# Seven products in place of eight for the middle group's second products, and one block's running sum kept in DRAM

## The chip, the core and the metric

One NeuronCore of a Trainium2 chip runs the whole kernel. The engines are TensorE (PE, matrix products), VectorE (DVE), ScalarE (ACT), GpSimd (POOL) and SyncE (SP, which issues most DMAs). SBUF is the working memory, PSUM holds what PE writes, DRAM is the main memory. The metric is the device time of one execution in microseconds (us), the median of several runs; lower is better.

## The reference

Three steps follow each other; the output is that of the last.

```python
# attention with decay: 2 batches, 8 heads, 768 tokens, 64 per head
state = gamma[None, :, None, None] * state + np.einsum('bhd,bhe->bhde', k[:, :, t], v[:, :, t])
y[:, :, t] = scale * np.einsum('bhd,bhde->bhe', q[:, :, t], state)
...
# first layer: x is 1536 x 512, w_gate and w_val 512 x 1536, w_out 1536 x 512
xn = x / rms * rms_g
g = xn @ w_gate
silu = g * (1.0 / (1.0 + np.exp(-g)))
x2 = (silu * (xn @ w_val)) @ w_out
...
# second layer: w_in is 512 x 2048, w_out 2048 x 512
h = x2 @ w_in
out = np.maximum(0.01 * h, h) @ w_out
```

## The kernel before

**Numbers in two parts.** The weights come in 64 bits and are converted on the chip, by ACT and DVE, to 32 bits and split into a high and a low part (the operations "P", "1" to "4", "H", "L" of `open_unit`). Every operand of a product is such a pair, and a product is three matmuls: high by high, high by low, low by high. A product of one column of 128 features with one block of 512 tokens is 12 matmuls of 128 x 512.

**Tiling.** The 1536 tokens are three blocks, b = 0, 1, 2. The features between two matrices go by columns f of 128, 12 in the first layer and 16 in the second. Columns go in groups of four: `groups` 0 to 2 are the first layer (kinds "gvo": w_gate, w_val, w_out), 3 to 6 the second (kinds "ip": w_in, w_out). First products (g, v, i) make a column's features; second products (o, p) take these features through w_out and add over a group's columns in four PSUM banks. At a group's end the banks go to SBUF.

**Seven products in place of eight.** Blocks 1 and 2 and two neighbouring columns form a 2 x 2 scheme in which seven products of sums replace eight (`quad` for first products, `seventh` for second ones). It needs sums and differences of weights (units named `sg4`, `sv4`, ...: "1" to "4", "H", "h", "L", "l" in `open_unit`), of inputs (`follow`), and additions of results (`put` in `seventh`). A product is then half as long: six matmuls. First products use it from column 2 of the first layer on. Second products use it in the groups of `seven`: before the change the last four, that is the second layer alone. The first layer's second products go the direct way: `down` makes one column by one block, `accumulate` adds over the group, and `evac1` empties the banks into `x2acc` (L660 by ACT in the first group, L662 by DVE in the others). When the last group is done, `evac1` queues the splitting of x2 into high (ACT, L665) and low parts (DVE, L668) in `sums`, from which two are taken at each step.

**Order.** `plan` writes out the order of all steps; a step's products and `later` work follow it. `run` takes the steps one by one; after each it makes the high and low parts of the next two columns (`upper`, `lower`, L611 and L619), and converts weights as long as estimated clocks of DVE and ACT stay behind that of PE. `wq` is the order in which weights are loaded and converted, `room` gives them one of 14 places, `free` and `used` give the place back. SP loads raw weights (L387) into three buffers, each free again when DVE has done step "3" (L468). Instructions then go to each engine's queue; a queue runs in order, but its order is not that of the text: what waits is placed later.

**What the change touches besides.** `more` is a tile of four 128 x 512 pieces. In the second layer `place` gives its pieces to block 0's features, and `evac2` copies block 0's sum of a group there (L796), which POOL adds to the output in DRAM (L800); `recall` reads the sum back before the last group's end (L816). `scratch` tiles, nine of them, hold the other features.

```python
    seven = set(range(len(groups) - SEVEN, len(groups)))
...
        for m in range(4):
            dst = acc[b][:, m, :]
            if gi == 0:
                nc.scalar.activation(out=dst, in_=banks[m], func=AF.Copy)
            else:
                nc.vector.tensor_tensor(out=dst, in0=banks[m], in1=dst, op=ALU.add)
```

Of the kernel before, what the change touches and what calls it, by code (L numbers as in the profile page):

```python
# [8 lines left out]
F32 = mybir.dt.float32  # L9
# [7 lines left out]
P = 128  # L17
# [9 lines left out]
LEFT = 2  # L27
HEAD = "dddd0"
OVER = 1.5
COST = {n: ("a", 1.2) if n == "P" else ("a", 0.54) if n == "H" else ("v", 0.34 if n in "12" else 0.6) for n in "P1234HL"}  # L30
COST_SUM = {n: ("a", 0.54) if n in "Hh" else ("v", 0.34 if n in "1234" else 0.6) for n in "123H4hLl"}
TWICE = "gvi"
SEVEN = 4
RAWS = 3
WARM = 7
# [27 lines left out]
def chain_kernel(ctx: ExitStack, tc: tile.TileContext, qk_t, kv, w1, w2, mask, qdec, kdec, sdec, rms_g, ident, out):  # L63
# [18 lines left out]
    scr = ctx.enter_context(tc.tile_pool(name="scr", bufs=SCRATCH))  # L82
    ps_acc = ctx.enter_context(tc.tile_pool(name="ps_acc", bufs=1, space=bass.MemoryType.PSUM))
    attn_pools = ctx.enter_context(ExitStack())
    score_pool = ctx.enter_context(ExitStack())
# [3 lines left out]
    sm = attn_pools.enter_context(tc.tile_pool(name="sm", bufs=4))  # L89

    mask_sb = const.tile([P, 2, NPAIR, CH], F32, name="mask_sb")
    qdec_sb = const.tile([P, NPAIR, CH], F32, name="qdec_sb")
# [256 lines left out]

    seven = set(range(len(groups) - SEVEN, len(groups)))  # L350

    def doubled(n, f):
        if n == "p":
            return any(f in groups[gi][1] for gi in seven)
        return n in TWICE and f"{n}{f}" not in PLAIN

    wq = []
    for gi, (kinds, fs) in enumerate(groups):
        pairs_of = [(n, f) for f in fs[::2] for n in kinds]
        if gi in seven:  # L360
            pairs_of.sort(key=lambda t: kinds.index(t[0]))
        for n, f in pairs_of:
            wq += [source(n, f), source(n, f + 1)]
            if doubled(n, f):
                wq.append((f"s{n}{f}", None))
# [25 lines left out]
    def open_unit():  # L391
# [12 lines left out]
        if src is None:  # L404
# [24 lines left out]

            if n == "p":  # L430
# [184 lines left out]
    def lower(key):  # L615
        if key in halves:
            x, h = halves.pop(key)
            l = gp.tile([P, 512], F32R, tag="gl", name="g{}_{}_{}l".format(*key))
            nc.vector.tensor_tensor(out=l, in0=x, in1=h.bitcast(F32), op=ALU.subtract)  # L619
            parted[key] = h, l  # L620
            spend("v", 0.6)
            if key[0] == "q":
                follow(key[1], key[2])
                spend("v", 0.6 if key[2] in (1, 3, 5, 6) else 0.0)
# [9 lines left out]
    def down(gi, f, b):  # L634
        kinds, fs = groups[gi]
        L = kinds[-1]
        key = (L, f, b)
        upper(key)
        lower(key)
        accumulate(L, gi, f, b, f == fs[0], f == fs[-1], L == "o" or b > 0)  # L640
        used(f"{L}{f}")
        if f == fs[-1]:
            banks = acc.pop("b")
            first = gi in (0, len(G1))
            by_copy = first or L == "p" and b == 0 and gi < len(groups) - 1
            later.append(("a" if by_copy else "v", 2.4, lambda: (evac1 if L == "o" else evac2)(gi, b, banks)))
        placed[0] = order.index(key) + 1

    def evac1(gi, b, banks):
        if gi == 0:  # L650
            acc[b] = xp.tile([P, 4, 512], F32, tag=f"acc{b}", name=f"x2acc{b}")
        last = gi == len(G1) - 1
        own = range(2, 4) if b == 2 else range(4)
        if last:
            x2h[b] = xp.tile([P, 4, 512], F32R, tag=f"xh{b}", name=f"x2h{b}")
            x2l[b] = xp.tile([P, 4, 512], F32R, tag=f"xl{b}", name=f"x2l{b}")
        for m in range(4):
            dst = acc[b][:, m, :]
            if gi == 0:
                nc.scalar.activation(out=dst, in_=banks[m], func=AF.Copy)  # L660
            else:
                nc.vector.tensor_tensor(out=dst, in0=banks[m], in1=dst, op=ALU.add)  # L662
        if last:
            def high(m):
                nc.scalar.activation(out=x2h[b][:, m, :], in_=acc[b][:, m, :], func=AF.Copy)  # L665

            def low(m):
                nc.vector.tensor_tensor(  # L668
                    out=x2l[b][:, m, :], in0=acc[b][:, m, :], in1=x2h[b][:, m, :].bitcast(F32), op=ALU.subtract
                )  # L670

            highs, lows = ([lambda m=m, do=do: do(m) for m in own] for do in (high, low))
            if b == 2:
                one, two = slice(0, 2), slice(2, 4)
                ops = sums_of(
                    acc, x2h, x2l, acc[1][:, one], acc[1][:, two], x2h[2][:, one], x2l[2][:, one], extra()[:, two]
                )
                first_of = [lambda i=i: [ops[n]() for n in (f"{i}", f"h{i}")] for i in range(4)]
                sums.extend(first_of[:2] + [ops["l1"]] + highs + [ops["l0"]] + lows)
                sums.extend([first_of[2], ops["l2"], first_of[3], ops["l3"]])  # L680
            else:
                sums.extend(highs + lows)

# [6 lines left out]

    def gather(gi):
        for f in groups[gi][1][::2]:
            t = {(k, b): made.pop(("p", f + k, b)) for k in range(2) for b in (1, 2)}
            made["q", f, 1], made["q", f, 3], made["q", f, 2] = t[0, 1], t[1, 2], t[1, 1]
            turns[f] = t

    turns = {}
    touched = set()

    def follow(f, n):  # L700
        t = turns[f]

        def less(out, in0, in1):
            nc.vector.tensor_tensor(out=out, in0=in0, in1=in1, op=ALU.subtract)

        if n == 1:
            less(t[0, 1], t[0, 2], t[0, 1])
            made["q", f, 5] = t[0, 1]
        elif n == 5:
            less(t[0, 1], t[1, 2], t[0, 1])  # L710
            made["q", f, 6] = t[0, 1]
        elif n == 6:
            less(t[0, 1], t[1, 1], t[0, 1])
            made["q", f, 4] = t[0, 1]
        elif n == 3:
            less(t[0, 2], t[1, 2], t[0, 2])
            made["q", f, 7] = t[0, 2]

    def seventh(gi, n, f):
        fs = groups[gi][1]  # L720
        key = ("q", f, n)
        if n == 1 and f == fs[0]:
# [6 lines left out]
        unit, half, side, start, (b, row) = SIDES[n]  # L729
        names = f"p{f}", f"p{f + 1}", f"sp{f}", f"sp{f + 1}"  # L730
        w = wt[names[unit]]
# [21 lines left out]
        if f != fs[-2]:  # L753
            return
        banks = acc[side]
        fresh = gi == len(G1) and (b, row) not in touched
        touched.add((b, row))
        if b not in y2:
            y2[b] = xp.tile([P, 4, 512], F32, tag=f"acc{b}", name=f"y2acc{b}")

        def put():
            for m in range(2):
                dst = y2[b][:, 2 * row + m, :]
                if fresh:
                    nc.scalar.activation(out=dst, in_=banks[m], func=AF.Copy)
                else:
                    nc.vector.tensor_tensor(out=dst, in0=banks[m], in1=dst, op=ALU.add)
# [116 lines left out]
    def place(n, key, own=None):  # L884

        if n == "v":
            return gates.pop(key)
        if n == "i" and key[1] == 0:
            return extra()[:, key[0] % 4, :]
        return scratch(f"{n}{key[0]}_{key[1]}") if own is None else own  # L890
# [45 lines left out]
    def quad(n, f):  # L936
# [5 lines left out]
        def kept_sum(m, src):  # L942
            def put():
                q[m] = scratch(f"{n}{m}_{f}")
                nc.scalar.activation(out=q[m], in_=src, func=AF.Copy)
# [53 lines left out]
    def plan():  # L999
# [12 lines left out]
        for gi, (kinds, fs) in enumerate(groups):  # L1012
# [19 lines left out]
            if first:  # L1032
                for n in HEAD:
                    if n == "d":
                        fill.pop(0)()
                    else:
                        f = fs[int(n)]
                        put((f"i{f}",), lambda f=f: whole("i", f, 0, x2h, x2l))
            if gi in seven:
                for f in fs[::2]:  # L1040
                    own = [fill.pop(0) for _ in range(min(2, len(fill)))]
                    for i7, (keys, step) in enumerate(quad("i", f)):
                        put(keys, step)
                        if i7 in BEHIND[2] and own:
                            own.pop(0)()
                wholes = [lambda f=f: put((f"i{f}",), lambda: whole("i", f, 0, h, l)) for k, f in enumerate(fs) if not first or str(k) not in HEAD]
                for n, more in zip((1, 5, 6, 3, 7, 2, 4), (1, 0, 1, 0, 1, 0, 1)):
                    for f in fs[::2]:
                        order.append(("q", f, n))
                        keys = (f"p{f}", f"p{f + 1}", f"sp{f}", f"sp{f + 1}")[SIDES[n][0]], "half"  # L1050
                        put(keys, lambda n=n, f=f, gi=gi: seventh(gi, n, f))
# [235 lines left out]
```

## Time and profile before

| | us |
|---|---|
| median of 3 runs | 582.85 (582.84 to 583.4) |
| the profiled execution | 583.3 |
| its span, first to last instruction | 581.3 |
| PE busy | 571.3 (98%) |
| DVE busy | 505.8 (87%) |
| ACT busy | 355.9 (61%) |
| POOL busy | 26.6 (5%) |

The profile is of one execution, and its own time is the one to compare with its span; around the span lie 2.0 us. TensorE's granted clock was 1.00 throughout. Attention takes the first 60 us or so, the first layer's products lie between about 70 and 338 us (the middle group between 141.5 and 234), the second layer's between 338 and 578. A busy time says how long an engine had an instruction in it, not that it worked at its best; "L" with a number is a line of the kernel printed above.

### The profile page before, as it was taken

The numbers are of one execution on the slowest core, as the hardware profiler recorded it, in microseconds if no ns is written. First come the engines' busy times: TensorE is split into PE (matmuls) and PEld (weight loads), VectorE is DVE, ScalarE is ACT, GpSimd is POOL, SyncE is SP. The second block draws the span as 40 slices with busy tenths as digits, with TensorE's granted clock in tenths as the row PEclk, the third lists the DMA queues.
The fourth block names the chain that finished last, engine by engine and source line by source line (L and its number), as shares of the span: only waits on it lengthen the run. The fifth ranks groups of instructions, "written<-read, shape, count | busy, mean of one in ns | idle before, by whom it ended". The sixth has DMA issues, their size and how long they took to land.

```text
span 581.3 us, 8448 instructions
## 1 busy us (share of the span) xinstructions
PE 571.3 (98%) x3107; PEld 471.1 (81%) x3107; DVE 505.8 (87%) x921; ACT 355.9 (61%) x652; POOL 26.6 (5%) x28
## 2 busy tenths in 40 slices
PE   7899999999999999999999999999999999999997
PEld 4788788888888888888888878888888888888885
DVE  4899999999578579697688999999999999997793
ACT  2689656776565464554564667877856885676330
POOL 2332100000000000000000000000000020002000
PEclk9999999999999999999999999999999999999999
DMA  8991240433222221221411111113411353111545
GB/s 327 408 392 59 73 144 1 145 110 115 67 73 73 72 74 31 78 72 38 144 37 36 38 36 37 57 53 108 173 39 43 109 142 78 36 37 19 127 85 133
DMA packets 34072, 56.97 MB, mean 98 GB/s; under 512 B 19184, under 2 KB 19312, under 8 KB 34032
## 3 DMA queue, kind: packets, MB, share of 16 engines
q1 hardware_dynamic: 32736, 54.34, 28.9%
q0 software_dynamic: 1152, 2.10, 2.5%
q8 instruction: 24, 0.39, 0.3%
q14 instruction: 16, 0.13, 0.1%
q10 hardware_dynamic: 144, 0.00, 0.0%
HBM read 50.14 MB, written 6.29 MB: 97 GB/s over the span
## 4 chain that ended last, share of the span: by engine, by line
PE 88%; DMA 6%; DVE 3%; ACT 2%; issue 1%; SPq 0%; POOL 0%; DVEq 0%; POOLq 0%; ACTq 0%
PE ao L603 17%; PE iX L931 8%; PE ap L603 7%; PE X L738 7%; PE i L574 7%; PE v L574 7%; PE g L574 6%; PE Z L738 6%; PE vX L931 5%; PE gX L931 5%; PE iZ L931 4%; PE vZ L931 2%; PE gZ L931 2%; DMA qkv<-in_qk_t 2%; PE iY L931 2%; DMA qkv<-in_kv 2%
## 5 line engine op out<-in xcount | busy, mean ns | idle before, releaser
L603 PE MATMUL ap<-w_p,gp_0h 128*128 128x512 f32 x128 | 39.4, 389 | 0.0
L574 PE MATMUL g<-xh,w_g 128*128 128x512 f32 x128 | 31.8, 390 | 0.0
L574 PE MATMUL i<-x2h,w_i 128*128 128x512 f32 x128 | 31.8, 389 | 0.0
L574 PE MATMUL v<-xh,w_v 128*128 128x512 f32 x128 | 31.7, 390 | 0.0
L603 PE MATMUL ao<-go_0h,w_o 128*128 128x512 f32 x96 | 31.5, 389 | 0.0
L603 PE MATMUL ao<-go_2h,w_o 128*128 128x512 f32 x96 | 31.1, 390 | 0.1
L603 PE MATMUL ao<-go_1h,w_o 128*128 128x512 f32 x96 | 30.5, 389 | 0.0
L800 POOL DMA_DIRECT2D out<-more x8 | 7.2, 1078 | 461.7 <-ACT more L796 461.5
L574 PEld LDWEIGHTS g<-xh,w_g 128*128 128x128 f32 x128 | 23.9, 188 | 5.2 <-issue 0.2
L574 PEld LDWEIGHTS i<-x2h,w_i 128*128 128x128 f32 x128 | 24.0, 188 | 5.0
L603 PEld LDWEIGHTS ap<-w_p,gp_0h 128*128 128x128 f32 x128 | 24.0, 188 | 5.0
L574 PEld LDWEIGHTS v<-xh,w_v 128*128 128x128 f32 x128 | 24.0, 188 | 4.9
L603 PE MATMUL ap<-w_p,gp_0l 128*128 128x512 f32 x64 | 24.9, 389 | 0.0
L879 DVE TENSOR_TENSOR g<-v,g 128x512 f32<-128x512 f32 x16 | 10.9, 688 | 14.5 <-PE v L574 14.5
L869 ACT ACTIVATE more<-i 128x512 f32<-128x512 f32 x16 | 9.5, 594 | 21.5 <-PE i L574 21.5
L603 PEld LDWEIGHTS ao<-go_2h,w_o 128*128 128x128 f32 x96 | 18.0, 188 | 4.2 <-issue 0.5
L603 PEld LDWEIGHTS ao<-go_0h,w_o 128*128 128x128 f32 x96 | 18.0, 188 | 3.7
L603 PEld LDWEIGHTS ao<-go_1h,w_o 128*128 128x128 f32 x96 | 18.0, 188 | 3.7
L931 PE MATMUL iZ<-x2h,w_si 128*128 128x512 f32 x64 | 20.3, 391 | 0.0
L931 PE MATMUL iX<-th,w_si 128*128 128x512 f32 x64 | 19.8, 391 | 0.0
L662 DVE TENSOR_TENSOR x2acc<-ao,x2acc 128x512 f32<-128x512 f32 x24 | 15.5, 686 | 4.1 <-PE ao L603 4.1
L603 PE MATMUL ao<-go_2l,w_o 128*128 128x512 f32 x48 | 18.7, 389 | 0.0
(294 smaller groups left out, 1730.8 us busy)
## 6 DMA issues: line engine op xcount, KB each, us to landing
raw_i<-in_w SPq DMA_DIRECT2D x16, 512.0 KB, 3.7
raw_p<-in_w SPq DMA_DIRECT2D x16, 512.0 KB, 3.7
raw_g<-in_w SPq DMA_DIRECT2D x12, 512.0 KB, 3.6
raw_v<-in_w SPq DMA_DIRECT2D x12, 512.0 KB, 3.6
raw_o<-in_w SPq DMA_DIRECT2D x12, 512.0 KB, 4.1
qkT<-in_qk_t SPq DMA_DIRECT2D x7, 512.0 KB, 6.9
kv<-in_kv SPq DMA_DIRECT2D x7, 512.0 KB, 8.1
qkv<-in_qk_t SPq DMA_DIRECT2D x5, 512.0 KB, 10.6
```

What stands on the lines that cost most here:

```text
L574: nc.tensor.matmul(out=dst, lhsT=lhs, rhs=rhs, start=(n == 0), stop=(n == len(pairs) - 1), skip_group_check=True)
L603: nc.tensor.matmul(out=acc["b"][m], lhsT=lhs, rhs=rhs, start=(start and n == 0), stop=(stop and n == 2))
L662: nc.vector.tensor_tensor(out=dst, in0=banks[m], in1=dst, op=ALU.add)
L738: nc.tensor.matmul(out=acc[side][m], lhsT=lhs, rhs=rhs, start=(start and f == fs[0] and k == 0), stop=(f == fs[-2] and k == 2), skip_group ...
L800: nc.gpsimd.dma_start(out=rows, in_=dst, accum_op=ALU.add)
L869: nc.scalar.activation(out=a, in_=x, func=AF.Prelu, alpha=0.01)
L879: nc.vector.tensor_tensor(out=a, in0=x, in1=a, op=ALU.mult)
L931: nc.tensor.matmul(out=dst, lhsT=lhs, rhs=rhs, start=(start and n == 0), stop=(n == 5), skip_group_check=True)
```

## The change

The middle group of the first layer (group 1, columns 4 to 7) joins `seven`, so that its second products for blocks 1 and 2 are made as seven products of sums. Its four columns of w_out get sums (`so4`, `so6`), its weights are ordered with w_out last, and `plan` gets a branch of its own for it: four `quad`s, the two columns' seven second products one kind after the other, with block 0's first products between them; block 0's second products go into the next group. The keys of such products are ("r", f, n) in this layer and ("q", f, n) in the second.

For block 0, the sum of x2 over the groups is no longer kept in SBUF. After each of the three groups ACT copies the banks to `more`; after the first SP writes them to DRAM tiles `held`, after the second and the third POOL adds them there, and after the third SP reads them back into `more`, from which x2's high and low parts are made. Since `more` is there from the first group on, block 0's features of columns 4 to 11 are put there as well, and some kept sums of column 6. `HEAD` is only moved.

```diff
+SEVEN1 = (1,)
...
+    held = [dram.tile([P, 512], F32, name=f"held{i}") for i in range(4)]
...
-    seven = set(range(len(groups) - SEVEN, len(groups)))
+    seven = set(range(len(groups) - SEVEN, len(groups))) | set(SEVEN1)
+
+    def of_seven(n, f):
+        return any(n == groups[gi][0][-1] and f in groups[gi][1] for gi in seven)
...
-        if n == "p":
-            return any(f in groups[gi][1] for gi in seven)
+        if n in "op":
+            return of_seven(n, f)
...
-            pairs_of.sort(key=lambda t: kinds.index(t[0]))
+            pairs_of.sort(key=lambda t: t[0] == kinds[-1])
...
-            if key[0] == "q":
-                follow(key[1], key[2])
+            if key[0] in "qr":
+                follow(*key)
...
-            by_copy = first or L == "p" and b == 0 and gi < len(groups) - 1
+            by_copy = gi == 0 or b == 0 and gi < len(groups) - 1
...
+        acc[0] = extra()
+        for m in range(4):
+            t = acc[0][:, m, :]
+            nc.scalar.activation(out=t, in_=banks[m], func=AF.Copy)
+            if gi == 0:
+                nc.sync.dma_start(out=held[m], in_=t)
+            else:
+                nc.gpsimd.dma_start(out=held[m], in_=t, accum_op=ALU.add)
+            if last:
+                nc.sync.dma_start(out=t, in_=held[m])
         if last:
+            high, low = x2_parts(0)
+            sums.extend([lambda m=m, do=do: do(m) for do in (high, low) for m in range(4)])
...
-                dst = y2[b][:, 2 * row + m, :]
+                dst = total[b][:, 2 * row + m, :]
...
-        if n == "i" and key[1] == 0:
+        if key[1] == 0 and (n == "i" or key[0] >= G1[0]):
             return extra()[:, key[0] % 4, :]
...
-                q[m] = scratch(f"{n}{m}_{f}")
+                if n == "v" and f % 4 == 2 and of_seven("o", f):
+                    q[m] = extra()[:, 3 if m == "u2" else 2, :]
+                else:
+                    q[m] = scratch(f"{n}{m}_{f}")
...
-            if gi in seven:
+            if gi in seven and L == "o":
+                wholes = [lambda n=n, f=f: put((f"{n}{f}",), lambda: whole(n, f, 0, xh, xl)) for f in fs for n in kinds[:-1]]
+                for f in fs[::2]:
+                    for n in kinds[:-1]:
+                        own = [(fill or wholes).pop(0) for _ in range(2)]
+                        for i7, (keys, step) in enumerate(quad(n, f)):
+                            put(keys, step)
+                            if i7 in BEHIND[2] and own:
+                                own.pop(0)()
+            elif gi in seven:
...
+            if gi in seven:
                 for n, more in zip((1, 5, 6, 3, 7, 2, 4), (1, 0, 1, 0, 1, 0, 1)):
                     for f in fs[::2]:
-                        order.append(("q", f, n))
+                        order.append((AS[L], f, n))
```

## Rows read from the trace of the kernel before

**Rows 1.** The page's first part: busy time, share of the span, instructions.

```profile
PE 571.3 (98%) x3107; PEld 471.1 (81%) x3107; DVE 505.8 (87%) x921; ACT 355.9 (61%) x652; POOL 26.6 (5%) x28
```

**Rows 2.** Waits for PE, 160 to 560 us: the heading, nothing under it.

```profile
engine line waited for: us in total, times, longest us
```

**Rows 3.** Busy time in windows (start:end length); the heading names the columns.

```profile
core 0: us, PE busy (x) PEld busy (x) DVE busy (x) ACT busy (x) POOL busy (x), PEclk, DMA share, GB/s
141.50:201.30 59.80, 59.80 (x265) 49.54 (x264) 40.01 (x73) 34.04 (x60) 0.00 (x0) 1.00 0.27 84
201.30:234.00 32.70, 32.70 (x146) 27.08 (x145) 29.16 (x54) 16.45 (x28) 0.00 (x0) 1.00 0.20 52
234.00:309.00 75.00, 75.00 (x333) 62.12 (x332) 56.75 (x103) 40.84 (x70) 0.00 (x0) 1.00 0.23 76
309.00:326.50 17.50, 17.50 (x78) 14.25 (x76) 16.50 (x30) 8.98 (x15) 0.00 (x0) 1.00 0.04 10
326.50:340.00 13.50, 13.37 (x60) 11.00 (x60) 13.24 (x24) 6.66 (x12) 0.00 (x0) 1.00 0.21 67
340.00:366.50 26.50, 26.50 (x117) 21.41 (x116) 26.26 (x42) 21.18 (x37) 0.00 (x0) 1.00 0.07 20
```

**Rows 4.** The chain of waits, 300 to 345 us: start, length, what.

```profile
318.43 8.16 PE ao L603 x36
...
326.72 11.17 PE ao L603 x48
```

**Rows 5.** Timeline of DVE, 309 to 319 us: start, length, instruction, count.

```profile
309.63 2.05 DVE L662 TENSOR_TENSOR x2acc<-ao,x2acc 128x512 f32<-128x512 f32 x3 [2.04 <-PE ao L603]
...
312.20 0.69 DVE L662 TENSOR_TENSOR x2acc<-ao,x2acc 128x512 f32<-128x512 f32 x1
312.80 0.68 DVE L619 TENSOR_TENSOR go_1l<-gs,go_1h 128x512 fp32r<-128x512 f32 x1
```

**Rows 6.** Groups of DVE's instructions, 400 to 460 us: busy us, mean ns.

```profile
L418 DVE TENSOR_TENSOR wa_p<-wa_p,wa_p 128x256 f32<-128x256 f32 x6 | 2.5, 418 | 0.0
```

**Rows 7.** Timeline of ACT, 310 to 320 us; idle time before in brackets.

```profile
310.36 1.31 ACT L665 ACTIVATE x2h<-x2acc 128x512 fp32r<-128x512 f32 x2 [0.81 <-DVE x2acc L662]
311.67 0.63 ACT L611 ACTIVATE go_1h<-gs 128x512 fp32r<-128x512 f32 x1
312.21 1.34 ACT L665 ACTIVATE x2h<-x2acc 128x512 fp32r<-128x512 f32 x2
...
319.20 0.63 ACT L611 ACTIVATE go_1h<-g 128x512 fp32r<-128x512 f32 x1 [5.12 <-DVE g L879]
```

**Rows 8.** Timelines of ACT, POOL and SP, 530 to 549 us.

```profile
533.38 0.60 ACT L796 ACTIVATE more<-ap 128x512 f32<-128x512 f32 x1 [0.34 <-PE ap L603]
...
534.28 0.86 POOL L800 DMA_DIRECT2D out<-more  x1 [56.08 <-ACT more L796]
535.29 2.63 POOL L800 DMA_DIRECT2D out<-more  x3 [0.15 <-issue]
...
538.46 5.68 SPq L816 DMA_DIRECT2D partial<-out  x4
```

**Rows 9.** Timelines of DVE (211.5 to 214) and PE (257 to 257.3 us).

```profile
212.29 0.68 DVE L484 TENSOR_TENSOR w_v<-wa_v,w_v 128x512 fp32r<-128x512 f32 x1
...
257.07 0.61 PE L931 MATMUL vX<-xh,w_v 128*128 128x512 f32 x2
```

**Rows 10.** DMA issues, 543.7 to 544.2 us: KB, us to landing.

```profile
partial<-out SPq DMA_DIRECT2D x1, 256.0 KB, 2.8
```

**Rows 11.** Timeline of SP's queue, 60 to 345 us.

```profile
304.31 31.21 SPq L387 DMA_DIRECT2D raw_i<-in_w  x3
```

**Rows 12.** Timelines of DVE and PE, 364.5 to 368 us.

```profile
366.42 0.69 DVE L425 TENSOR_TENSOR w_sp<-wa_p,w_sp 128x512 fp32r<-128x512 f32 x1
...
367.49 0.62 PE L738 MATMUL Z<-gq_5h,w_sp 128*128 128x512 f32 x2
```

**Rows 13.** Busy time in one window, 534.2 to 538 us; columns as in rows 3.

```profile
534.20:538.00 3.80, 3.80 (x19) 3.14 (x18) 3.73 (x8) 3.80 (x8) 3.49 (x4) 1.00 0.67 73
```

More of the change, by code (lines that the diff above doesn't have):

```diff
@@ L27 @@
 LEFT = 2
-HEAD = "dddd0"
 OVER = 1.5
@@ L33 @@
 SEVEN = 4
+SEVEN1 = (1,)
+HEAD = "dddd0"
 RAWS = 3
@@ L83, in chain_kernel @@
     ps_acc = ctx.enter_context(tc.tile_pool(name="ps_acc", bufs=1, space=bass.MemoryType.PSUM))
+    dram = ctx.enter_context(tc.tile_pool(name="dram", bufs=1, space=bass.MemoryType.DRAM))
     attn_pools = ctx.enter_context(ExitStack())
@@ L428, in low_part @@
                 return put
-            if n == "p":
+            if n in "op":
                 return key, None, {
@@ L649, in evac1 @@
     def evac1(gi, b, banks):
-        if gi == 0:
-            acc[b] = xp.tile([P, 4, 512], F32, tag=f"acc{b}", name=f"x2acc{b}")
         last = gi == len(G1) - 1
-        own = range(2, 4) if b == 2 else range(4)
+        if b:
+            if gi == 0:
+                acc[b] = xp.tile([P, 4, 512], F32, tag=f"acc{b}", name=f"x2acc{b}")
+            for m in range(4):
+                dst = acc[b][:, m, :]
+                if gi == 0:
+                    nc.scalar.activation(out=dst, in_=banks[m], func=AF.Copy)
+                else:
+                    nc.vector.tensor_tensor(out=dst, in0=banks[m], in1=dst, op=ALU.add)
+            if not last:
+                return
+            highs, lows = ([lambda m=m, do=do: do(m) for m in range(2 * b - 2, 4)] for do in x2_parts(b))
+            if b == 1:
+                sums.extend(highs + lows)
+                return
+            one, two = slice(0, 2), slice(2, 4)
+            ops = sums_of(acc, x2h, x2l, acc[1][:, one], acc[1][:, two], x2h[2][:, one], x2l[2][:, one], extra()[:, two])
+            both = [lambda i=i: [ops[n]() for n in (f"{i}", f"h{i}")] for i in range(4)]
+            sums.extend(both[:2] + [ops["l1"]] + highs + [ops["l0"]] + lows + [both[2], ops["l2"], both[3], ops["l3"]])
+            return
@@ L654, in evac1 @@
+        acc[0] = extra()
+        for m in range(4):
+            t = acc[0][:, m, :]
+            nc.scalar.activation(out=t, in_=banks[m], func=AF.Copy)
+            if gi == 0:
+                nc.sync.dma_start(out=held[m], in_=t)
[3 more added lines that the diff above has]
+                nc.sync.dma_start(out=t, in_=held[m])
         if last:
+            high, low = x2_parts(0)
+            sums.extend([lambda m=m, do=do: do(m) for do in (high, low) for m in range(4)])
@@ L655, in evac1, with x2_parts @@
+    def x2_parts(b):
+        if b not in x2h:
             x2h[b] = xp.tile([P, 4, 512], F32R, tag=f"xh{b}", name=f"x2h{b}")
             x2l[b] = xp.tile([P, 4, 512], F32R, tag=f"xl{b}", name=f"x2l{b}")
[L657 to L682, printed above, removed]
@@ L684, in chain_kernel, with high, low @@
+        def high(m):
+            nc.scalar.activation(out=x2h[b][:, m, :], in_=acc[b][:, m, :], func=AF.Copy)
+        def low(m):
+            nc.vector.tensor_tensor(
+                out=x2l[b][:, m, :], in0=acc[b][:, m, :], in1=x2h[b][:, m, :].bitcast(F32), op=ALU.subtract
+            )
+        return high, low
     SIDES = {
@@ L691, in gather, with follow @@
     def gather(gi):
+        L = groups[gi][0][-1]
+        q = AS[L]
         for f in groups[gi][1][::2]:
-            t = {(k, b): made.pop(("p", f + k, b)) for k in range(2) for b in (1, 2)}
-            made["q", f, 1], made["q", f, 3], made["q", f, 2] = t[0, 1], t[1, 2], t[1, 1]
-            turns[f] = t
+            t = {(k, b): made.pop((L, f + k, b)) for k in range(2) for b in (1, 2)}
+            made[q, f, 1], made[q, f, 3], made[q, f, 2] = t[0, 1], t[1, 2], t[1, 1]
+            turns[q, f] = t
+    AS = {"o": "r", "p": "q"}
     turns = {}
     touched = set()
-    def follow(f, n):
-        t = turns[f]
+    def follow(q, f, n):
+        t = turns[q, f]
         def less(out, in0, in1):
@@ L707, in follow @@
             less(t[0, 1], t[0, 2], t[0, 1])
-            made["q", f, 5] = t[0, 1]
+            made[q, f, 5] = t[0, 1]
         elif n == 5:
             less(t[0, 1], t[1, 2], t[0, 1])
-            made["q", f, 6] = t[0, 1]
+            made[q, f, 6] = t[0, 1]
         elif n == 6:
             less(t[0, 1], t[1, 1], t[0, 1])
-            made["q", f, 4] = t[0, 1]
+            made[q, f, 4] = t[0, 1]
         elif n == 3:
             less(t[0, 2], t[1, 2], t[0, 2])
-            made["q", f, 7] = t[0, 2]
+            made[q, f, 7] = t[0, 2]
     def seventh(gi, n, f):
         fs = groups[gi][1]
-        key = ("q", f, n)
+        L = groups[gi][0][-1]
+        key = (AS[L], f, n)
         if n == 1 and f == fs[0]:
@@ L729, in seventh @@
         unit, half, side, start, (b, row) = SIDES[n]
-        names = f"p{f}", f"p{f + 1}", f"sp{f}", f"sp{f + 1}"
+        names = f"{L}{f}", f"{L}{f + 1}", f"s{L}{f}", f"s{L}{f + 1}"
         w = wt[names[unit]]
@@ L755, in seventh @@
         banks = acc[side]
+        total = y2 if L == "p" else acc
         fresh = gi == len(G1) and (b, row) not in touched
-        touched.add((b, row))
-        if b not in y2:
+        if L == "p":
+            touched.add((b, row))
+        if b not in total:
             y2[b] = xp.tile([P, 4, 512], F32, tag=f"acc{b}", name=f"y2acc{b}")
@@ L943, in put @@
             def put():
-                q[m] = scratch(f"{n}{m}_{f}")
+                if n == "v" and f % 4 == 2 and of_seven("o", f):
+                    q[m] = extra()[:, 3 if m == "u2" else 2, :]
+                else:
+                    q[m] = scratch(f"{n}{m}_{f}")
                 nc.scalar.activation(out=q[m], in_=src, func=AF.Copy)
@@ L1045, in plan @@
                             own.pop(0)()
-                wholes = [lambda f=f: put((f"i{f}",), lambda: whole("i", f, 0, h, l)) for k, f in enumerate(fs) if not first or str(k) not in HEAD]
+                wholes = [lambda f=f: put((f"i{f}",), lambda: whole("i", f, 0, x2h, x2l)) for k, f in enumerate(fs) if not first or str(k) not in HEAD]
+            if gi in seven:
                 for n, more in zip((1, 5, 6, 3, 7, 2, 4), (1, 0, 1, 0, 1, 0, 1)):
                     for f in fs[::2]:
-                        order.append(("q", f, n))
-                        keys = (f"p{f}", f"p{f + 1}", f"sp{f}", f"sp{f + 1}")[SIDES[n][0]], "half"
+                        order.append((AS[L], f, n))
+                        keys = (f"{L}{f}", f"{L}{f + 1}", f"s{L}{f}", f"s{L}{f + 1}")[SIDES[n][0]], "half"
                         put(keys, lambda n=n, f=f, gi=gi: seventh(gi, n, f))
```

## The prediction

> **What bounds the kernel now.** I read the page's busy times first: TensorE (PE) is busy for 571.3 us, 98% of the span of 581.3 [rows 1]. Busy time alone would not prove that PE sets the end, so the view of waits for PE between 160 and 560 us came next: it lists nothing under its heading, so no gap of PE there ends on another engine [rows 2]. The windows then say how near the others are. In the first layer's middle group (141.5 to 234 us) VectorE (DVE) is busy for 40.01 of 59.80 and 29.16 of 32.70 us, so 23.3 us idle; in the third group (234 to 309) it is idle for 18.3 us. From 309 on that ends: 1.0 us idle in 17.5, 0.26 in 13.5, 0.24 in 26.5 [rows 3]. So PE is the bound, and in the second layer DVE is a close second. Last, the chain of waits gives PE's price: 36 second products, one after the other, take 8.16 us, which is 0.2267 us each and 2.72 us for twelve [rows 4]. A matmul taken out of the steady part is worth 0.2267 us, as long as nothing else gets late.
>
> The profiled execution took 583.3 us, 2.0 more than its span, and 0.45 more than the median, 582.85. I work in the span and move the result by +1.55 to compare it with the median. A measurement of this kernel can tell about 0.2%, 1.2 us, from no change.
>
> **What goes.** For blocks 1 and 2 the middle group's second products are now 4 columns of 2 blocks of 12 matmuls, 96. As seven products for each of two pairs they are 7 x 2 x 6 = 84. Block 0 keeps its 48, and the number of first products is the same; only their order changes. So 12 matmuls go: **-2.72 us** [rows 4].
>
> **What is added to DVE and ScalarE (ACT).** DVE starts a 512-wide two-input operation every 0.60 us (312.20 to 312.80) although each lasts 0.69 [rows 5]; a 256-wide one takes 0.42 [rows 6].
> - Sums of w_out for two pairs: 2 x (4 x 0.42 + 2 x 0.60) = 5.8 us of DVE; four high parts at 0.63 on ACT [rows 7].
> - Fourteen sets of parts where there were eight: 6 x 0.60 = 3.6 us of DVE, 6 x 0.63 = 3.8 of ACT [rows 7]. Eight differences that make the next input: 8 x 0.60 = 4.8.
> - Fourteen additions from PSUM where there were eight: 3.6 us.
> - Block 0's four additions in this group go to ACT as copies (4 x 0.60 [rows 8]): -2.4 us of DVE.
>
> That is +15.4 us of DVE in a stretch with 23.3 - 2.7 = 20.6 us idle [rows 3]. It fits if it can be spread, and weights give room to spread it: the low part of w_val's column 8 is written at 212.29 and first used at 257.07, 44 us later [rows 9]. I cost it at nothing. If the cover were gone, each us of overflow is a us of PE. ACT is busy for about half of both stretches [rows 3] and takes its additions.
>
> **What moves: block 0's sum.** After the first group SyncE (SP) writes four tiles to DRAM: four more issues behind ACT's copies, ahead of some weight loads; weights converted 44 us ahead [rows 9] cover that, and with three times 1 MB more the DMA engines, busy for 0.22 to 0.27 of these stretches [rows 3], have room. After the middle group POOL adds four tiles there; its queue has nothing else to do then. The tile `more` is next written by ACT when g of column 8 is ready, two steps (1.36 + 2.72 = 4.1 us) after the last bank; the first addition has landed by then if it goes like the case below (5.1 us after the copy's start, 3.0 after the last bank, which comes three times 0.68 us behind the first). After the third group the full round trip stands in the way of x2's parts: copy by ACT, addition by POOL, read back by SP, and only then the high part (ACT) and the low part (DVE).
>
> The trace has one such round trip, at the start of the last group's second products. ACT's first copy starts at 533.38, POOL issues from 534.28 to 537.92, SP issues the first read at 538.46, which is when the first addition has landed, and the last at 543.8 [rows 8]; that read landed 2.8 us later [rows 10]. From first copy to last landing: 546.6 - 533.4 = 13.2 us. At the end of the first layer the first bank is free at 309.63, where DVE now begins its additions [rows 5]. So the last tile would be back at 322.8, its high part done at 323.5 and its low part at 324.2. The first product that needs them starts when the 48 matmuls from 326.72 are over, at 337.89 [rows 4]: 13.7 us later. The latency is hidden. SP's queue can add to it: between 304.31 and 335.52 SP issues three weight loads, each held until DVE is done with a buffer [rows 11], and a read that stands behind one of them could come some 10 us later (31.21 / 3); that too is inside the 13.7.
>
> What is not surely hidden is the queue behind it. ACT and DVE work in order, and the high and low parts wait in their queues. On ACT the next conversion behind is that of column 11 for block 1 at 319.20; ACT was idle for 5.12 us before it, so a hold until 319.2 is free [rows 7]. PE wants this operand in the third of the three sets from 318.43, at 323.87 [rows 4]. If it stood behind all four low parts, it would be ready at 324.2 + 0.60 (product with the gate) + 0.63 + 0.69 = 326.1: a stall of 2.2 us. On DVE, in the worst order, only the four low parts run between 313.4 and 324.2, so 10.8 - 2.4 = 8.4 us are lost; of these the four additions that left (2.4) and the idle 1.5 us [rows 3] pay back 3.9, and 4.5 are left as lateness. DVE then stays full, and at 366.42 it writes the low part of a sum of the second layer's w_out which PE uses at 367.49, 0.4 us after it is done [rows 12]. That would stall PE by 4.1 us. The two stalls don't add up, since a stalled PE lets DVE catch up. At the other end the price is 0: the order of a queue is not that of the text, since a conversion for the next products stood between two pairs of x2's high parts (311.67 on ACT), and its low part between DVE's other work (312.80) [rows 5, 7]. A gain beyond the matmuls is excluded, since PE waits for nothing there [rows 2]. Between 0 and 4.1 I take 0.4, near the lower end, because both engines had other ready work in these rows and the next operand's slot on ACT was idle.
>
> POOL's four issues in this round trip took 3.64 us in all, beside a DVE that was busy for 3.73 of 3.80 us [rows 13]. The Trainium skill's page "SBUF — State Buffer", in its box on DMAs issued by GpSimd and in "Who interferes with whom", states that some DVE operations shut GpSimd out of a shared port pair, and gives 3.1 us in place of 0.62 for such a transfer. By the rows the trip is 13.2 us and the sum holds; by an estimate from that page's figure the four issues would take 12.4 us, the trip 8.8 more, and the sum would be a loss if the queues are held. The trace does not agree that it bites here; the last rival works out its like from rows.
>
> **The sum.** Span 581.3 - 2.72 + 0.4 = 579.0; this execution 581.0; against the median **580.5 us**.
>
> **The rivals.**
> 1. *The read-back holds the queues and eats the gain.* For it: the four accumulations land late in the one case there is, and DVE has 0.4 us to spare in the second layer [rows 8, 12]. Against it: other work was placed in between [rows 7]. Price 1.5 to 4.1, middle 2.8: 582.85 - 2.72 + 2.8 = 582.9 us, no change that can be told.
> 2. *DVE becomes the bound in the new second products (slower).* Their stretch is 7 x 2.72 + 4 x 2.72 = 29.9 us. DVE has 14 + 8 + 14 operations at 0.60, and four more for block 0, 24.0 us; the next group's weights that fall there now (two conversions of 3 x 0.60 + 2 x 0.42 and two pairs of sums of 2.9) are 11.1: 35.1 in 29.9. If they come ahead of the parts, PE waits 5.2 us: 585.3 us. It turns the sign from 3.9 us on. Against it: 19.8 us idle just before [rows 3], the 44 us of slack [rows 9], and the same pattern in the second layer, which keeps PE full at a DVE that is full too [rows 2, 3].
> 3. *POOL is shut out and the tiles come late.* If DVE let only one addition through at a time, each would take the 4.2 us from POOL's first issue to SP's first read, the last would be done 16.7 us after the first issue and not 9.5 (543.8), and the trip would be 7.2 us longer [rows 8]. With the conversions held behind it, each us is a us of PE: 2.2 + 7.2 = 9.4, so 589.5 us; it turns the sign once the last tile is back 1.7 us later than 322.8. Against it: four issues in 3.64 us beside a full DVE [rows 8, 13].
>
> **How the numbers follow.** My forecast, a stall of 0 to 1.5 us: 0.64 (its own range 580.0 to 581.6). Rival 1: 0.21. Rival 2: 0.12. Rival 3: 0.03. Faster by over 0.2% is the first, 0.64; within 0.2% rival 1, 0.21; slower 0.15. The range begins at 579.8, all 2.72 us gained and 0.3 for the measurement, and reaches through most of rival 1, to 583.8.
>
> **What would show it.** Right: the third group's first product begins 2.72 us earlier; DVE fuller in the middle group (about 85 of 90 us) and no wait of PE there; the read of the four tiles landed 10 to 14 us after the first copy, and the first product of the second layer still without a wait. Wrong: waits of PE for DVE at the sums' products (rival 2), a gap of PE in the last 15 us of the first layer or a late sum of weights soon after (rival 1), POOL issues of 2 us and more (rival 3).

## The result, and the profile after

The changed kernel takes **586.85 us** (median of 6 runs, 585.71 to 590.77), the one before 582.87 beside it: a ratio of 1.0075 with a 95% interval of 1.0047 to 1.0103. It is slower by 4.0 us, where I had forecast 2.35 us less. The profiled execution took 586.72 us with a span of 584.7, 3.4 more than that of before in each. One execution in the experiments below, of 821.8 us at a mean granted clock of 0.66, was in a slower state of the chip and is left out of the times.

The page's first part, which answers to [rows 1], shows 12 matmuls less, as meant, and PE busy 1.2 us longer all the same:

```profile
PE 572.5 (98%) x3095; PEld 471.1 (81%) x3095; DVE 513.6 (88%) x945; ACT 364.5 (62%) x670; POOL 33.7 (6%) x36
```

Fewer matmuls that are busy for longer means that some of them ran slower. Not all of that costs time: in the first 62 us, mostly attention, PE is busy for 58.16 us where it had 56.14 before (the kernels of the experiments have 56.6 to 58.2 there), and the middle group begins no later, at 141.05 for 141.47. The view of waits for PE, 130 to 570 us, was empty before [rows 2] and now has three waits, each met once:

```profile
engine line waited for: us in total, times, longest us
PE ao L610 <- DVE x2acc L666: 2.4, 1, 2.4
PE ao L610 <- ACT go_1h L618: 1.6, 1, 1.6
PE ao L610 <- DVE go_1l L626: 0.2, 1, 0.2
```

The windows (columns as in rows 3) say where. The middle group, now 141.5 to 231.3, and the third, to 306.3, are full of PE work; only the last 35 us of the first layer are not, and windows of 1 us within them show the granted clock down to 0.50, half speed:

```profile
141.50:201.30 59.80, 59.78 (x264) 49.19 (x263) 44.27 (x83) 33.77 (x59) 0.00 (x0) 1.00 0.22 66
201.30:231.30 30.00, 30.00 (x134) 24.86 (x133) 29.66 (x55) 16.34 (x28) 0.00 (x0) 1.00 0.06 18
231.30:306.30 75.00, 75.00 (x332) 62.10 (x332) 63.36 (x121) 46.96 (x82) 3.99 (x4) 1.00 0.42 120
306.30:323.80 17.50, 15.69 (x69) 12.45 (x68) 9.07 (x17) 8.21 (x15) 3.51 (x4) 1.00 0.58 120
323.80:340.00 16.20, 13.76 (x54) 10.90 (x53) 14.33 (x27) 7.73 (x14) 0.00 (x0) 0.89 0.11 35
...
329.00:330.00 1.00, 1.00 (x5) 0.80 (x4) 1.00 (x3) 1.00 (x3) 0.00 (x0) 0.73 0.86 262
330.00:331.00 1.00, 1.00 (x4) 0.71 (x4) 1.00 (x3) 1.00 (x3) 0.00 (x0) 0.50 0.28 102
331.00:332.00 1.00, 1.00 (x4) 0.81 (x3) 1.00 (x2) 0.17 (x1) 0.00 (x0) 0.50 0.00 0
```

In 306.3 to 323.8 DVE is busy for 9.07 of 17.5 us, where it had 16.50 of 17.5 before [rows 3]: it stands idle in the stretch in which PE begins to wait. The timelines of POOL, SP, ACT and DVE tell what it waits for. First the round trip:

```profile
307.69 3.51 POOL L685 DMA_DIRECT2D held<-more  x4 [53.56 <-ACT more L681]
...
311.75 5.79 SPq L687 DMA_DIRECT2D more<-held  x4
```

Then ACT, the engine that both begins and ends it:

```profile
306.80 2.64 ACT L681 ACTIVATE more<-ao 128x512 f32<-128x512 f32 x4
...
317.37 1.82 ACT L698 ACTIVATE x2h<-more 128x512 fp32r<-128x512 f32 x3 [6.53 <-DMA more<-held]
319.95 0.63 ACT L698 ACTIVATE x2h<-more 128x512 fp32r<-128x512 f32 x1 [0.77 <-DMA more<-held]
321.95 0.63 ACT L618 ACTIVATE go_1h<-g 128x512 fp32r<-128x512 f32 x1 [1.36 <-DVE g L908]
```

And DVE, behind ACT:

```profile
318.03 1.90 DVE L701 TENSOR_TENSOR x2l<-more,x2h 128x512 fp32r<-128x512 f32 x3 [4.01 <-ACT x2h L698]
320.62 0.69 DVE L701 TENSOR_TENSOR x2l<-more,x2h 128x512 fp32r<-128x512 f32 x1 [0.69 <-ACT x2h L698]
321.23 0.68 DVE L908 TENSOR_TENSOR g<-vX,g 128x512 f32<-128x512 f32 x1
...
322.62 0.68 DVE L626 TENSOR_TENSOR go_1l<-g,go_1h 128x512 fp32r<-128x512 f32 x1
...
327.74 2.48 DVE L666 TENSOR_TENSOR x2acc<-ao,x2acc 128x512 f32<-128x512 f32 x4
```

The trip itself went as forecast: first copy at 306.80, last tile back at 319.9, 13.1 us (forecast 13.2), and x2's parts are needed at 341. But column 11's gated product for block 1 (`g`, L908) stands in DVE's queue behind all four low parts: it starts at 321.23, its high part is done at 322.6. Everything behind it is late too, and so is the emptying of block 1's banks (327.74). PE's timeline shows both ends of this, and then the slow matmuls:

```profile
322.63 0.50 PE L610 MATMUL ao<-go_1h,w_o 128*128 128x512 f32 x1 [1.58 <-ACT go_1h L618]
323.36 0.50 PE L610 MATMUL ao<-go_1l,w_o 128*128 128x512 f32 x1 [0.23 <-DVE go_1l L626]
...
328.57 0.47 PE L610 MATMUL ao<-go_2h,w_o 128*128 128x512 f32 x1 [2.44 <-DVE x2acc L666]
...
330.10 1.05 PE L610 MATMUL ao<-go_2h,w_o 128*128 128x512 f32 x2
330.96 0.63 PE L610 MATMUL ao<-go_2l,w_o 128*128 128x512 f32 x1
```

From 330.10 to 330.96 two matmuls start, 0.43 us each in place of 0.227. The chain of waits, which answers to [rows 4], closes the account: the last 48 products of the first layer begin 1.85 us later than before and last 1.60 us longer, 3.45 in all, which is the 3.4 us of the span.

```profile
328.57 12.77 PE ao L610 x48
341.34 2.72 PE i L581 x12
```

### The profile page after: what moved, and what is told of

Read it like the earlier page. It is cut to its first block, busy times and chain, and to the rows that moved or that the text cites. A ratio compares the mean times of both kernels' runs of the same rounds, so it can differ in the third digit from the quotient of the medians.

```text
span 584.7 us, 8511 instructions
## 1 busy us (share of the span) xinstructions
PE 572.5 (98%) x3095; PEld 471.1 (81%) x3095; DVE 513.6 (88%) x945; ACT 364.5 (62%) x670; POOL 33.7 (6%) x36
## 4 chain that ended last, share of the span: by engine, by line
PE 50%; issue 30%; DMA 10%; DVE 5%; ACT 3%; POOL 1%; SPq 0%; POOLq 0%; ACTq 0%; DVEq 0%
PE iX L960 7%; PE ap L610 7%; PE i L581 7%; PE X L765 7%; PE Z L765 6%; PE iZ L960 4%; PE ao L610 3%; DMA held<-more 3%; PE v L581 2%; PE g L581 2%; DMA qkv<-in_qk_t 2%; PE iY L960 2%; DMA qkv<-in_kv 2%; DMA kv<-in_kv 1%; DMA mask_sb<-in_mask 1%
## 5 line engine op out<-in xcount | busy, mean ns | idle before, releaser
L610 PE MATMUL ao<-go_2h,w_o 128*128 128x512 f32 x64 | 21.7, 409 | 2.4 <-DVE x2acc L666 2.4
L610 PE MATMUL ao<-go_1h,w_o 128*128 128x512 f32 x64 | 20.6, 391 | 1.6 <-ACT go_1h L618 1.6
L685 POOL DMA_DIRECT2D held<-more x8 | 7.5, 1280 | 235.1 <-ACT more L681 235.1
L610 PE MATMUL ao<-go_0l,w_o 128*128 128x512 f32 x48 | 18.7, 389 | 0.0
L538 ACT ACTIVATE wb_i<-raw_i 128x512 int32<-128x512 uint32 x16 | 10.8, 673 | 11.7 <-DVE wa_p L484 4.5
L197 DVE TENSOR_TENSOR a<-sc,mask_sb 128x1024 f32<-128x1024 f32 (+1 forms) x13 | 14.5, 1135 | 3.4 <-PE sc L185 3.0
L610 PEld LDWEIGHTS ao<-go_2h,w_o 128*128 128x128 f32 x64 | 12.8, 200 | 5.7 <-issue 2.8
```

What stands on the lines that cost most here:

```text
L197: nc.vector.tensor_tensor(out=s["a"][:, j], in0=s["sc"][:, j], in1=mask_sb[:, j], op=ALU.mult)
L538: nc.scalar.activation(out=m, in_=low.bitcast(U32), func=AF.Copy, scale=2.0 ** -29)
L610: nc.tensor.matmul(out=acc["b"][m], lhsT=lhs, rhs=rhs, start=(start and n == 0), stop=(stop and n == 2))
L685: nc.gpsimd.dma_start(out=held[m], in_=t, accum_op=ALU.add)
```

## The experiments

Theory A: the instructions that wait for the read-back hold ACT's and DVE's queues. Theory B: the sevens' own load on DVE. Theory C: the transfers themselves. The kernel before, on the same chips, took 583.0 (the first four), 582.81 (the next four) and 583.01 us (the last two).

**The DRAM sum alone.** Block 0's sum stays in DRAM, the middle group's second products are direct again.

```diff
-SEVEN1 = (1,)
+SEVEN1 = ()
```

> Only block 0's sum goes through DRAM; the middle group's second products stay eight, so no matmul is saved. Theory A (ACT's and DVE's queues are held behind the read-back at the end of the first layer: 4.2 us of waits of PE, then 3.4 us at half clock): the whole loss without the 2.7 us of gain, 586.85 + 2.7 = 589.6 us (588.5 to 590.5), with the same two waits of PE. Theory B (the seven products' 15 us more of DVE make it late): no loss, 582.9. Theory C (the transfers themselves, their share of the DMA engines): 589.6, as A.

588.91 us (median of three), ratio 1.0102 [1.0087, 1.0116]. The loss is there without the sevens, 5.9 us: B falls. Where its waits lie is read in the last experiment, the same kernel.

**No round trip.** The writes, the additions and the reads in DRAM are left out, so block 0's x2 is the third group's share alone.

```diff
-            if gi == 0:
-                nc.sync.dma_start(out=held[m], in_=t)
-            else:
-                nc.gpsimd.dma_start(out=held[m], in_=t, accum_op=ALU.add)
-            if last:
-                nc.sync.dma_start(out=t, in_=held[m])
```

> The seven products stay; block 0's sum is not carried at all: ACT copies the banks as before, but the writes, additions and reads of DRAM are left out, so that block 0's x2 is the third group's share alone. A and C: 582.87 - 2.72 = 580.1 us (579.5 to 581.0), no wait of PE at the end of the first layer, clock 1.00 there. B: still slower than before, about 586.

580.69 us, ratio 0.9959 [0.9948, 0.9971]. PE waits for nothing and its clock stays at 1.00 in the layers. With the sevens and their load on DVE kept, that is 2.3 us less than before.

**Read early.** The sum of two groups is read at column 10's second product, into the place of block 0's low part, which is free then; DVE adds the third group's banks to it.

```diff
+        if key == ("o", sum(G1) - 2, 0):
+            x2_parts(0)
+            for m in range(4):
+                nc.sync.dma_start(out=x2l[0][:, m, :].bitcast(F32), in_=held[m])
...
+            if last:
+                nc.vector.tensor_tensor(out=t, in0=banks[m], in1=x2l[0][:, m, :].bitcast(F32), op=ALU.add)
+                continue
```

> The sum of the first two groups is read back into the place of x2's low part as soon as the first layer's last use of it is over (column 10's step), and DVE adds the third group's banks to it, as in the kernel before. The third group's four additions by POOL go, the reads stay but come about 6 us before they are needed. A: nothing is held, 580.1 us (579.5 to 581.0), faster than both. B: about 586. C: between, 583 to 587, since 4 MB of the 5 MB of transfers stay.

580.81 us, ratio 0.9961 [0.994, 0.9981], faster than both kernels. No wait of PE from 130 us on. Its chain of waits gives the gain without any loss: the 48 products begin 2.83 us earlier than before [rows 4]. Of this, 0.28 us is a lead from before the middle group, whose first products begin at 141.35 for 141.63.

```profile
323.89 11.14 PE ao L610 x48
335.03 2.72 PE i L581 x12
```

**The same trip, the parts behind.** The DMAs stay as in the changed kernel. Only block 0's high and low parts are placed behind column 11's parts for block 1, in each queue. (The edit also lets `run` take four of them a step, in place of two, while more than eight wait.)

```diff
+            if key == ("o", sum(G1) - 1, 1):
+                marks["a"] = getattr(ins, "ins", ins)
...
+                    with tc.issue_after(marks[n]):
+                        do(m)
```

> The round trip stays as it is, and only the order in ACT's and DVE's queues changes: block 0's high and low parts stand behind the conversion of column 11 for block 1, which PE waited for. A: most of the loss goes, 580.1 to 581.5 us. B and C: unchanged, 586 to 587, since neither the load nor the transfers change.

580.83 us, ratio 0.9964 [0.9952, 0.9977]. The transfers are those of the changed kernel and the loss is gone: A holds, C falls. ACT's timeline shows the order. The conversion that the changed kernel made at 321.95 comes at 316.49, ahead of x2's parts, and so do three operations on weights (314.21 to 315.94). ACT waits 0.37 us for the tiles, where it had waited 6.53:

```profile
316.49 0.62 ACT L619 ACTIVATE go_1h<-g 128x512 fp32r<-128x512 f32 x1
317.48 1.71 ACT L713 ACTIVATE x2h<-more 128x512 fp32r<-128x512 f32 x3 [0.37 <-DMA more<-held]
```

On DVE the gated product `g` and the emptying of block 1's banks come early too:

```profile
315.56 0.68 DVE L923 TENSOR_TENSOR g<-vX,g 128x512 f32<-128x512 f32 x1
...
323.04 2.48 DVE L673 TENSOR_TENSOR x2acc<-ao,x2acc 128x512 f32<-128x512 f32 x4
```

**Work in PE's gaps.** To see whether the half clock comes from PE standing still, the two gaps get 6 and 10 matmuls whose result nobody uses.

```diff
+        n = {("o", sum(G1) - 1, 1): 6, ("o", G1[0] + G1[1], 2): 10}.get(key, 0)
...
+                nc.tensor.matmul(out=fill, lhsT=w[:, 0, :P], rhs=w[:, 0, :], start=True, stop=True)
```

> The changed kernel with 16 further matmuls of TensorE whose result nobody reads: 6 ahead of column 11 for block 1 and 10 ahead of column 8 for block 2, where PE waited 1.6 and 2.4 us. They take 16 x 0.227 = 3.6 us of the 4.2 us of waits. If the half clock after the waits (3.4 us of the profile, worth 1.7 us) is what a PE that stands still brings, the clock stays at 1.00 there and the time falls to 585.1 us (584.4 to 585.8) in spite of more work. If those matmuls were slow for another cause (operands, weights), it stays at 586.9 or rises.

587.64 us, ratio 1.0080 [1.0067, 1.0093]: my 585.1 was wrong. On the clock the answer is clear, it stays at 1.00 (windows):

```profile
324.00:326.00 2.00, 2.00 (x10) 1.64 (x10) 1.97 (x5) 1.48 (x4) 0.00 (x0) 1.00 0.00 0
326.00:330.00 4.00, 3.24 (x15) 2.40 (x14) 4.00 (x8) 2.22 (x5) 0.00 (x0) 1.00 0.36 111
330.00:334.00 4.00, 4.00 (x20) 3.28 (x19) 3.97 (x8) 2.91 (x6) 0.00 (x0) 1.00 0.07 25
```

So the slow matmuls came from the gaps. The run changes more than PE's work, though: on DVE an operation on weights (L484, 327.64) now comes ahead of the emptying of block 1's banks, which starts at 328.25 and not at 327.74. The time did not come back with the clock. This kernel begins the second layer at 340.1, 1.1 us earlier than the changed one, and then waits 0.9 us for a part that ACT makes (`th`, L881). By the two chains of waits the same six products begin at 391.23 here and at 390.53 in the changed kernel: a lead of 1.1 us has become a lag of 0.7. The wait took half of this, and matmuls that start apart before 366 the rest. Another 0.4 us goes later, and the span is 1.1 us longer in the end. That a slower PE had been giving DVE time to catch up is my reading of this, and it is not shown.

**Only the low parts behind.** As with the parts behind, but the high parts stay where the changed kernel has them.

```diff
+            sums.extend([lambda m=m: high(m) for m in range(4)])
+            held_back.extend([lambda m=m, do=behind("v", low): do(m) for m in range(4)])
```

> The high parts of block 0 stay early in ACT's queue, and only the low parts on DVE stand behind column 11's. If DVE's queue is the one whose hold costs (its lateness gave the longer wait, 2.4 us), most of the loss goes: 581 to 583 us. If ACT's hold costs as much by itself, column 11's conversion still waits for the read-back there: 584 to 586.

585.52 us, ratio 1.0052 [1.0038, 1.0065]. One held engine is enough: ACT stands 6.64 us at `x2h`, DVE waits for ACT's conversions, and PE waits 1.1 and 2.2 us at the same two places. Its clock stays at 1.00.

```profile
317.32 1.96 ACT L714 ACTIVATE x2h<-more 128x512 fp32r<-128x512 f32 x3 [6.64 <-DMA more<-held]
...
319.83 0.69 DVE L432 TENSOR_TENSOR w_si<-wa_i,w_si 128x512 fp32r<-128x512 f32 x1 [4.71 <-ACT w_si L428]
```

**A longer trip.** SP copies each tile once more, from DRAM to DRAM, ahead of the read; the rest as in the changed kernel.

```diff
-                nc.sync.dma_start(out=t, in_=held[m])
+                nc.sync.dma_start(out=held2[m], in_=held[m])
+                nc.sync.dma_start(out=t, in_=held2[m])
```

> The changed kernel with a longer trip: after POOL's additions SP copies the four tiles to other DRAM tiles and reads these, some 4 us more. If each us of the trip is a us of PE, 590 to 592 us. If only the order of the queues counts, which puts the parts behind other work when the trip is longer, about the same as the changed kernel, 585 to 588.

586.3 us, ratio 1.0057 [1.0045, 1.007], no slower than the shorter trip. The queues came out in another order, with column 11's conversion after two high parts in place of four (323.06). There is one wait of PE, 2.8 us, and a clock of 0.50 from 324 to 330. The order of the queues counts here, and not the length of the trip alone.

**The longer trip with the parts behind.** Both edits together.

> The longer trip together with the parts queued behind column 11's conversion. If latency costs nothing as long as nothing needed stands behind it, 580.5 to 582.5 us, 4 us of trip more for less than 2 of time. If the trip itself costs, 4 us above the run with the short trip in that order: 584.8.

587.63 us, ratio 1.008 [1.0068, 1.0093], a miss: I had expected the cure to hold. Column 11 is in time, but the tiles now come so late that the parts hold what stands behind them, block 2's conversion on ACT and the emptying of block 1's banks on DVE (327.24; 323.04 with the short trip):

```profile
316.63 0.62 ACT L620 ACTIVATE go_1h<-g 128x512 fp32r<-128x512 f32 x1
320.75 0.63 ACT L715 ACTIVATE x2h<-more 128x512 fp32r<-128x512 f32 x1 [3.50 <-DMA more<-heldb]
322.24 1.29 ACT L715 ACTIVATE x2h<-more 128x512 fp32r<-128x512 f32 x2 [0.85 <-DMA more<-heldb]
323.43 0.61 ACT L620 ACTIVATE go_2h<-gu 128x512 fp32r<-128x512 f32 x1
```

PE waits once, 4.4 us, for those banks, and the 48 products behind, part of them at half clock, take 13.90 us (11.17 before, rows 4). Placing the parts behind one instruction cures only as much lateness as that place has room for.

**The longer trip with early reads.** The same additional copies ahead of the early reads.

```diff
+                nc.sync.dma_start(out=held2[m], in_=held[m])
+                nc.sync.dma_start(out=x2l[0][:, m, :].bitcast(F32), in_=held2[m])
```

> The same four additional copies from DRAM to DRAM that made the trip longer in the other kernels, now ahead of reads that are issued a column earlier. In the kernel with early reads the four reads were issued from 297.96 us on and their tiles were first used at 306.81; the copies made the reads some 3 us later in the other kernel, so they should still land first. If it is the order behind a late read that costs (my theory), nothing is held: 580.5 to 581.3 us, no wait of PE over 0.3 us at the end of the first layer. If a longer trip costs something wherever it stands (SP's queue, the transfers), it is slower than 580.8 by 1 us and more: 582 to 585.

586.69 us, ratio 1.0062 [1.0047, 1.0077], a miss on the time. The end of the first layer is clean (from 280 us on the chain is PE alone), but the copies depend on nothing but the middle group's additions, so SP issued them from 256.75 on, 47 us ahead of the reads, as soon as these had landed, and ahead of a load of weights. That load left at 260.22 (254.69 with early reads alone) beside the copies, and ACT stood at it:

```profile
266.38 0.66 ACT L539 ACTIVATE wb_i<-raw_i 128x512 int32<-128x512 uint32 x1 [6.85 <-DMA raw_i<-in_w]
266.94 0.62 ACT L488 ACTIVATE w_v<-wa_v 128x512 fp32r<-128x512 f32 x1
267.46 0.62 ACT L619 ACTIVATE go_0h<-more 128x512 fp32r<-128x512 f32 x1
267.98 0.58 ACT L984 ACTIVATE vu<-vX 128x512 f32<-128x512 f32 x1
```

PE waited 3.1 us for that `vu`, which empties a bank, and ran at a clock of 0.50 from 268 to 274, which cost another 2.9 us: by the chain, 24 products from 268.62 on took 8.36 us for 5.44. It is the same mechanism with other work, and it does not test what I meant it to test: the reads were no later against their use than in the kernel with early reads.

**The DRAM sum alone, its waits.** The kernel of the first experiment, run again.

> Block 0's sum in DRAM alone, the middle group's second products direct as before, once more for a profile. By my theory the trip costs what it costs with the sevens: PE waits for column 11's product of block 1 and for the emptying of block 1's banks, 4 to 5 us in two gaps, TensorE's granted clock under 1.00 for some 3 us after the second, and the first product of the second layer starts at 337.9 + 6 = 344 us; the time 588.3 to 589.5. If the sevens' load on DVE made it, there are no such gaps and the time is 583.

588.86 us (587.51 to 593.18), ratio 1.0124 [1.008, 1.0167]. The waits are at the places of the changed kernel:

```profile
PE ao L610 <- ACT go_1h L618: 1.8, 1, 1.8
PE ao L610 <- DVE x2acc L666: 0.8, 1, 0.8
...
PE ao L610 <- DVE go_1l L626: 0.2, 1, 0.2
```

They are 2.8 us and not the 4 to 5 I had expected, and the half clock came in another place, after the first gap (0.61 and 0.53 in the windows from 326 to 330). The slower products fill part of the second gap, which is 1.6 us shorter. The last 48 products begin at 331.14, 4.42 us later than before, and its profiled execution took 4.5 us longer than before's 583.3. This is less than the 6.3 us that the hold costs in the changed kernel's profile (4.68 + 1.60, below), and this execution was among the shorter ones; by the medians the two lose about the same, 5.9 and 6.2 us (4.0 and the 2.2 not gained).

## Why the prediction was wrong

**The step that failed** is "Between 0 and 4.1 I take 0.4". The worst order of my own bounds came: column 11's product behind all four low parts. I had read the order of the queues from an execution without the trip [rows 5, 7], where nothing in these queues waited long, and took it for a sign that other work would be put in between. It says nothing on what is put where once the parts depend on a DMA. Undoing this order (the parts behind) takes the loss away.

**The bounds were too low as well.** The stall on ACT's side was priced about right, 2.2 us for a measured 1.58 + 0.23. But I had followed DVE's lateness only to a sum of weights at 366, and it stopped PE 40 us earlier, at a place that I had not looked at: the emptying of block 1's banks, without which block 2's products can't begin. That cost 2.44 us more, so "The two stalls don't add up, since a stalled PE lets DVE catch up" was wrong. Against the kernel with the parts behind, DVE's `g` was 5.7 us late (321.23 for 315.56) and the banks' emptying still 4.7 (327.74 for 323.04). With a remainder of 0.43, which fits the single matmuls that start apart, the 48 products begin 4.68 us later than with early reads (328.57 for 323.89).

**A term was missing: TensorE's clock.** I costed a gap at its length. After 2.4 us without work PE soon ran at half clock, 1.2 of 2.4 GHz, and the 48 products took 1.60 us more (12.77 for 11.17). The sum as it was, from the chains: -2.83 + 4.68 + 1.60 = +3.45 us. It is rival 1 of the text, at 6.3 us in place of 1.5 to 4.1, and therefore beyond the range.

**What held.** The term of -2.72 us measured -2.55 from the middle group on in the chain with early reads (the -2.83 less the lead of 0.28; some 0.18 went to matmuls that start apart at 144 to 147), and 2.2 to 2.3 us show in the medians of the three kernels without the hold. The trip of 13.2 us measured 13.1. The cost of nothing for the sevens' work on DVE held: no wait of PE in the middle group. DVE's instructions are 24 more, as the four lists add up with block 0's eight additions gone, but not where I put them. In the middle group there are 138 for 127 before, in the third 121 for 103, and DVE is busy for 73.9 of 89.8 us, where I had said about 85 of 90. Rivals 2 and 3 did not come. The tile `more` was not quite in time after the middle group: where I had the first addition landed before ACT writes the tile again, ACT waited 1.22 us for it, until 256.23. PE did not notice.

**POOL.** At the first layer's end its four issues took 3.51 us, as before [rows 13], but DVE was busy for only 1.21 of these. After the middle group they took 3.99 us beside a DVE that was never idle (the second line is the window of these 3.99 us, columns as in rows 3), so POOL was not shut out there either:

```profile
250.14 3.99 POOL L685 DMA_DIRECT2D held<-more  x4 [181.49 <-ACT more L681]
...
250.14:254.13 3.99, 3.99 (x19) 3.30 (x18) 3.99 (x10) 3.99 (x9) 3.99 (x4) 1.00 0.59 131
```

The 3.1 us for one such transfer, from the Trainium skill's page "SBUF — State Buffer" that I weighed, do not show in either place: POOL's issues took 0.85 to 1.75 us each. The four additions at the first layer's end landed 4.0 to 7.4 us after their issue, those of the middle group up to 9.2. The Trainium skill's page "DMA: Bandwidth & Descriptors" ("Anatomy of one DMA") gives 2.0 us plus the bytes over 436 GB/s for a DMA that POOL issues, by which I estimate 2.6 us for these 256 KB; the measurement decides, and these accumulations took longer. How much of that is the accumulation, and how much that four of them share the DMA engines, is open.

## What to carry to other kernels

A long latency with enough time before its use is hidden only if nothing is queued behind the instruction that waits for it: for each wait on a DMA, follow the in-order queue behind it, on each engine that waits, and price the worst order unless the program fixes a better one. Fetch early, into a place that is free already, so that the last step is a local operation; placing the waiting instruction later helps only up to the room there is, and a DMA freed of its dependence moves ahead of loads that others wait for. Price a gap of PE of about 2 us at more than its length: where half clock followed, it cost 1.6 us (after 2.4), 2.7 (after 4.4) and 2.9 (after 3.1) on top.

## What the hardware showed unexpectedly

Half clock followed gaps of 1.8 us (the DRAM sum alone), 2.4 (the changed kernel), 2.8, 3.1 and 4.4 us (the three longer trips), but not one of 2.2 us with only the low parts behind, so a gap of about 2 us does not decide it by its length alone (each is one profiled execution). In the longer trip the clock fell while PE still waited (0.60 in the window from 323 to 324, PE busy for 0.27 of it); in the changed kernel it fell only after PE had resumed at 328.57 (0.73 from 329 to 330). It lasted from 3 to 7 us in these rows and rose again while PE worked without waiting. Keeping PE busy with unused matmuls held the clock at 1.00 and saved nothing: the engines that feed PE were as late as before.
